# Hashed attention with two feed-forward blocks on one core: two weight slices converted at the attention's end, token differences in 2 KB halves, layer 3's first weight sums made in layer 2

## The chip, the cores and the metric

The kernel runs on one core of one Trainium2 chip. The metric is the device time of one execution in microseconds (us), the median over several runs; lower is better.

## The reference, cut to what matters

Everything is computed at fp32 accuracy. An attention over 16 heads (768 positions, 64 wide), in which a query sees only the keys of its hash bucket, gives the tokens `x` (1536 x 512); then four dense layers follow:

```
attn = softmax(where(q_bucket == k_bucket, q @ k.T / 8, -1e9)) @ v      # 2 x 8 heads
x = attn.transpose(0, 2, 1, 3).reshape(1536, 512)
h = max(max(x @ w1, x @ w2), x @ w3)          # layer 1: three 512 x 768
x = h @ w_out                                 # layer 2: 768 x 512
h = x @ w_in                                  # layer 3: 512 x 2048
g = where(h >= 1, h, where(h <= -1, 0, (h + 1)**2 / 4))
out = g @ w_out2                              # layer 4: 2048 x 512
```

## The kernel before, in words

**Matrix products.** An fp32 factor is held as two fp32r parts, hi and lo, and a product is three matmuls (hi·hi, hi·lo, lo·hi). A tile of 128 output features x 512 tokens with 256 inputs is therefore 6 matmuls of 128x512. Tokens lie in three blocks c = 0, 1, 2 of 512. PSUM banks come from a rotation of seven, `b0` to `b5` and `u_ps` (`bank`, `free`); the eighth, `pj_ps`, is scratch for the weights. Every engine takes its instructions in the order in which the program wrote them; an instruction that waits holds up all that stand behind it in its queue.

**Weights.** They arrive as 8-byte floats, in slices of 128 x 512 (512 KB), numbered in order of use: 0 to 17 for layer 1, 18 to 25 for layer 2 (384 wide), from 26 on for layers 3 and 4 in turn, two and two. `w_steps` converts one slice in steps: load of slice n+2 on SP (L196), Square on ACT (L211), four integer operations on DVE (L213, L218, L222, L226) that leave an fp32 number, on ACT the cast that makes hi (L234). The lo part is a subtraction on POOL (`w_low`, L268), issued when the next slice begins or when the slice is asked for. `w_tick(k)` makes k such steps; the calls of `w_tick`, strewn over the matrix work, are what sets the place of the steps in each queue. Of the raw 8-byte tiles there are two (`wr`), of the fp32 ones two (`wg2`).

**Pairs.** Slices 4 to 17 and those of layer 3 are taken two at a time by `pair_units`, which gets two slices x two blocks of tokens with seven products for eight, Strassen's way. It needs four sums of quarters of the two weight slices (s3, s2, s1, s4: `sr`, L245 to L250 on DVE), split into hi (ACT, L256) and lo (POOL, L258) by `sums_parts`, and four differences of tokens T1 to T4 (`x_d`; T4 overwrites a part of `x_hl`). When the next slice is the second of a pair and sums of an earlier pair are still to be split, `w_tick` stops; `w_state["open"]` says up to which pair sums may be split. Within a pair the matmuls come in groups of 6: product a; two groups of a plain block q; f = s3·T3; b += s2·T2 on top of a copy of a (L1056, ACT); a second product onto a; q; b += s1·T1; q; d; e. Between them ACT copies f to `x7` (L1067), DVE adds d = b + x7 (L1072), which must be through before s1 goes onto b, and ACT copies b to e (L1082) and to y (L1084), the first of which must be through before the product e.

**Order around the change.** A planner places the attention's work; at its end (some 195 to 207 us) hand-written code finishes the last pair of heads: row sums to `rt` (ACT, L594), `rt` to DRAM by a DMA from ACT's queue (L599), back as `rb` on all rows (SP, L605), the rows multiplied (`xr`, L614, DVE), then `x_hl` hi (L623, ACT) and lo (L627, DVE). Meanwhile PE runs the first units of layer 1 on the finished batch. Nine single units of layer 1 follow (`todo`, L1125 on; each ends in a copy or a maximum `h`, L967, L969), between which the 14 `steps` of the token differences run: four sums of two 128x1024 pieces (two on POOL, two on DVE, L1104), then `less` (DVE, L1027), casts (ACT, L1020) and lo parts (L1023, POOL or DVE). Then come the seven pairs `LEFT`, and layer 2: 12 units of 18 matmuls, whose results go straight to `x_hl` and to the token differences of layer 3 (L1163 to L1178). From 405.6 us on layers 3 and 4 run interleaved, pair i of layer 3 with the slices of pair i-1 of layer 4 (L1235), one `w_tick(2)` after each group of layer 3; g is made of r by ACT and DVE (L1201 to L1203), its hi by ACT (L1212), its lo by POOL (L1213).

Lines that carry another number after the change, in the rows of its order: L234 becomes L238, L256 L261, L594 L604, L599 L609, L605 L615, L1056 L1068, L1067 L1079, L1072 L1084, L1082 L1094, L1084 L1096, L1201 to L1212 become L1240 to L1251.

Of the kernel before, what the change touches and what calls it, by code (L numbers as in the profile page):

```python
# [8 lines left out]
F32 = mybir.dt.float32  # L9
# [104 lines left out]
def lsh_attention_moe_kernel(  # L114
# [85 lines left out]
    def w_steps(n):  # L200
# [16 lines left out]
        g2 = w_p.tile([128, 512], I32, tag="wg2", name="wg2", bufs=2)[:, 0:cols]  # L217
# [11 lines left out]
        yield  # L229
# [4 lines left out]
        nc.scalar.copy(out=w[:, 0, 0:cols], in_=f32(g2))  # L234
        splits[n] = w
        low_todo.append((n, w, g2, cols))
        g2s[n] = f32(g2)
# [28 lines left out]
    def w_low():  # L266
        for n, w, g2, cols in low_todo:
            nc.gpsimd.tensor_tensor(out=w[:, 1, 0:cols], in0=f32(g2), in1=f32(w[:, 0, 0:cols]), op=ALU.subtract)  # L268
        low_todo.clear()

    def w_tick(count=1):
        for _ in range(count):
            sums_tick()
            if w_state["gen"] is None:
                n = w_state["done"]
                if n >= NSL:
                    w_low()
                if n >= NSL or n >= w_state["base"] + (WBUFS if w_state["more"] else WEARLY):
                    return
                if n in pair_at and sums_todo:  # L280
                    return
                w_state["gen"] = w_steps(n)
# [37 lines left out]
    def attention(mlp_steps):  # L320
        with ExitStack() as ax, ExitStack() as sx:
# [610 lines left out]
    def mlp():  # L932
        with ExitStack() as mx:
# [11 lines left out]
            def free(b, full=True):  # L945
                banks.append(b[0])
                (whole.add if full else whole.discard)(b[0])
# [6 lines left out]
            def tok(c):  # L954
                return slice(c * TCH, (c + 1) * TCH)
# [48 lines left out]
            w_state["sums"] = mx.enter_context(tc.tile_pool(name="s", bufs=4))  # L1004
# [4 lines left out]
            low = [None] * 4  # L1009
            lk, rk, c0, c1 = slice(0, 2), slice(2, 4), tok(0), tok(1)  # L1010

            def lows():
                for m in (2, 1, 0, 3):
                    low[m] = w_state["sums"].tile([128, 2, TCH], F32, tag="s", name="raw")

            def d_parts(m, rows, eng):
                to = [x_d[:, m, p, rows] if m < 3 else x_hl[:, p, rows, c1] for p in range(2)]

                def hi():
                    nc.scalar.copy(out=to[0], in_=low[m][:, rows])  # L1020

                def lo():
                    eng.tensor_tensor(out=to[1], in0=low[m][:, rows], in1=f32(to[0]), op=ALU.subtract)  # L1023
                return hi, lo
# [12 lines left out]
            def pair_units(m, out_):  # L1037
# [6 lines left out]
                for x, (t, i) in dict(s3=(0, 0), s2=(0, 1), s1=(1, 0), s4=(1, 1)).items():  # L1044
                    left[x] = [tuple(s_[t][:, p, i, k * 128:(k + 1) * 128] for p in range(2)) for k in range(2)]
# [55 lines left out]
            with tc.tile_pool(name="h", bufs=1) as h_p:  # L1101
                hh["t"] = h_p.tile([128, 6, 2, NT], F32R, name="hh")
                lows()
# [3 lines left out]
                cut = [d_parts(m, lk, eng) for m, eng in enumerate((nc.gpsimd, nc.gpsimd, nc.vector, nc.gpsimd))]  # L1107
                steps = [
                    lambda: add(nc.gpsimd, 0, lk, c0),
                    lambda: add(nc.gpsimd, 3, rk, c0),  # L1110
                    lambda: add(nc.vector, 2, lk, c1),
                    lambda: add(nc.vector, 1, rk, c1),
                    lambda: less(low[0], low[2], low[0]),
                    lambda: less(low[2], low[1], low[2]),
                    cut[2][0],
                    lambda: less(low[1], low[1], low[0]),
                    cut[2][1],
                    cut[0][0],
                    cut[1][0],
                    lambda: less(low[3], low[3], low[1]),  # L1120
                    cut[1][1],
                    cut[0][1],
                ]

                todo = [(j, w, c) for j, w in ((0, 0), (0, 1), (0, 2), (1, 0)) for c in range(NTC) if (j, w, c) not in early or c]  # L1125
                for n, (j, w, c) in enumerate(todo):
                    l1(j, w, c, slice(S - TCH, TCH) if (j, w, c) in early else slice(0, TCH), 2 if n < 4 else 3)
                    for _ in range(3):
                        if steps:
                            steps.pop(0)()  # L1130
                    if not steps:
                        w_state["open"] = 1
                    if n + 1 == len(todo) or todo[n + 1][1] != w:
                        w_done(("1", j, w))
                for fn in steps:
                    fn()
                cut[3][0]()
                cut[3][1]()
# [11 lines left out]
                lows()  # L1150
                for j in range(4):
                    wts = [w_get(("2", j, g)) for g in range(2)]
                    i = j % 2
                    for c in ((2, 0, 1) if j == 0 else range(NTC)):
# [10 lines left out]
                        elif c == 0:  # L1165
                            raw = low[0 if j < 2 else 3][:, i]
# [3 lines left out]
                        elif j < 2:  # L1170
                            nc.scalar.copy(out=low[2][:, i], in_=pb)
                            less(low[0][:, i], low[2][:, i], low[0][:, i])
                        else:
                            t1, t2, t3, t4 = (t[:, i] for t in low)
                            one = slice(i, i + 1)
                            cut = [d_parts(m, one, eng) for m, eng in enumerate((nc.gpsimd, nc.gpsimd, nc.vector, nc.gpsimd))]
                            nc.scalar.copy(out=t2, in_=pb)
                            nc.scalar.copy(out=xh, in_=pb)  # L1178
                            less(t3, t2, t3)
                            cut[2][0]()  # L1180
                            less(xl, t2, f32(xh))
                            cut[2][1]()
                            less(t2, t2, t1)
                            less(t4, t4, t2)
                            for m in (0, 1, 3):
                                for fn in cut[m]:
                                    fn()
                        free(b)
                        w_tick(4)
                        if j == 3 and c == 1:  # L1190
                            w_state["open"] = len(LEFT) + 2
                    w_done(("2", j, 1))

            with tc.tile_pool(name="g", bufs=1) as g_p:
# [57 lines left out]
                for i in range(9):  # L1252
# [68 lines left out]
```

## Time and profile before

| | us |
|---|---|
| runs shown, median (lowest, highest) | 673.12 (672.02, 676.54) |
| the profiled execution | 671.09 |
| its span in the trace | 669.3 |
| granted TensorE clock, mean over the span | 0.987 of full speed |

The rows below come from the profiled execution. Its span starts with the first instruction; 1.8 us of the execution lie outside it. A matmul of 128x512 at full clock follows the one before after 227 ns (6 take 1.36 us, as the starts of consecutive groups in the trace show).

### The profile page before, as it was taken

The numbers are of one execution on the slowest core, as the hardware profiler recorded it, in microseconds if no ns is written. First come the engines' busy times: TensorE is split into PE (matmuls) and PEld (weight loads), VectorE is DVE, ScalarE is ACT, GpSimd is POOL, SyncE is SP. The second block draws the span as 40 slices with busy tenths as digits, with TensorE's granted clock in tenths as the row PEclk, the third lists the DMA queues.
The fourth block names the chain that finished last, engine by engine and source line by source line (L and its number), as shares of the span: only waits on it lengthen the run. The fifth ranks groups of instructions, "written<-read, shape, count | busy, mean of one in ns | idle before, by whom it ended". The sixth has DMA issues, their size and how long they took to land.

```text
span 669.3 us, 11587 instructions
## 1 busy us (share of the span) xinstructions
PE 645.2 (96%) x4323; PEld 513.4 (77%) x4323; DVE 495.6 (74%) x803; ACT 396.6 (59%) x740; POOL 352.8 (53%) x313
## 2 busy tenths in 40 slices
PE   7999999999999899889999998799999999999998
PEld 5668777778867677768888886588888888888886
DVE  5788989999863899878844477655786969696554
ACT  7687877887782344555443246778748374646440
POOL 6437547766322577657645255754646464645340
PEclk8999999999999989999999999899999999999999
DMA  6857787786333012231211211221211212121004
GB/s 189 224 122 185 198 213 182 199 247 153 92 112 81 32 64 95 94 95 55 71 49 47 64 63 59 68 94 64 64 63 64 89 37 94 36 92 63 1 0 189
DMA packets 27857, 66.99 MB, mean 100 GB/s; under 512 B 4165, under 2 KB 9125, under 8 KB 27801
## 3 DMA queue, kind: packets, MB, share of 16 engines
q1 hardware_dynamic: 27488, 66.21, 33.9%
q8 instruction: 34, 0.56, 0.3%
q14 instruction: 23, 0.18, 0.1%
q10 hardware_dynamic: 312, 0.04, 0.0%
HBM read 46.17 MB, written 3.19 MB: 74 GB/s over the span
## 4 chain that ended last, share of the span: by engine, by line
PE 79%; DVE 12%; ACT 4%; issue 3%; DMA 1%; POOL 1%; DVEq 0%; ACTq 0%; SPq 0%; POOLq 0%
PE b L308 24%; PE b L1235 18%; PE u_ps L308 7%; PE s_ps L449 6%; PE t_ps L482 5%; PE u_ps L543 5%; PE s_ps L452 5%; PE u_ps L510 3%; DVE raw L1027 2%; PE u_ps L1235 2%; PE pj_ps L425 2%; DVE pj_ps L213 1%; DVE wg L226 1%; DVE wg L218 1%; DVE pj_ps L222 1%
## 5 line engine op out<-in xcount | busy, mean ns | idle before, releaser
L459 DVE TENSOR_SCALAR_CACHE_REDUCE p<-s_ps 128x768 f32<-128x768 f32 x96 | 89.7, 951 | 13.3 <-PE s_ps L452 10.0
L474 ACT ACTIVATE p<-p,nm 128x768 f32<-128x768 f32 x96 | 89.7, 936 | 7.2 <-DVE p L459 6.7
L1213 POOL TENSOR_TENSOR g<-r,g 128x512 fp32r<-128x512 f32 x48 | 62.7, 1306 | 37.9 <-ACT g L1212 37.7
L449 PE MATMUL s_ps<-lo,q 128*128 128x384 f32 x192 | 72.5, 378 | 3.1 <-POOL lo L416 2.0
L308 PE MATMUL b<-x_d,s 128*128 128x512 f32 x270 | 68.6, 398 | 6.4 <-DVE u_ps L1072 2.6
L1235 PE MATMUL b<-wx,g 128*128 128x512 f32 x264 | 67.5, 393 | 4.5 <-ACT wx L234 3.3
L308 PE MATMUL b<-x_hl,wx 128*128 128x512 f32 x264 | 65.7, 393 | 1.5 <-ACT x_hl L1163 1.2
L308 PEld LDWEIGHTS b<-x_d,s 128*128 128x128 f32 x270 | 51.2, 192 | 19.6 <-DVE u_ps L1072 3.4
L452 PE MATMUL s_ps<-hi,q 76*128 76x384 f32 x192 | 66.1, 344 | 0.0
L213 DVE SCALAR_TENSOR_TENSOR pj_ps<-pj_ps,wr 128x512 f32<-128x512 f32 (+1 forms) x55 | 37.2, 677 | 37.5 <-ACT pj_ps L211 37.5
L1235 PE MATMUL b<-w,g 128*128 128x512 f32 (+1 forms) x264 | 64.6, 384 | 0.0
L234 ACT CAST wx<-wg 128x512 fp32r<-128x512 f32 (+1 forms) x32 | 19.4, 605 | 73.3 <-DVE wg L226 73.3
L1235 PEld LDWEIGHTS b<-wx,g 128*128 128x128 f32 x264 | 49.8, 189 | 15.7 <-ACT wx L234 3.7
L268 POOL TENSOR_TENSOR wx<-wg,wx 128x512 fp32r<-128x512 f32 (+1 forms) x32 | 40.7, 1273 | 39.3 <-ACT wx L234 36.1
L308 PEld LDWEIGHTS b<-x_hl,wx 128*128 128x128 f32 x264 | 50.1, 190 | 12.7 <-ACT x_hl L1163 1.7
L308 PE MATMUL b<-x_hl,w 128*128 128x512 f32 (+1 forms) x282 | 59.5, 363 | 0.0
L1242 DVE TENSOR_TENSOR acc<-b,acc 128x512 f32<-128x512 f32 (+1 forms) x77 | 51.6, 677 | 8.9 <-PE b L1235 8.9
L1235 PEld LDWEIGHTS b<-w,g 128*128 128x128 f32 x264 | 48.9, 188 | 9.9
L308 PEld LDWEIGHTS b<-x_hl,w 128*128 128x128 f32 x282 | 48.0, 189 | 8.8 <-issue 0.6
L449 PEld LDWEIGHTS s_ps<-lo,q 128*128 128x128 f32 x192 | 36.7, 191 | 21.3 <-DVE p L459 8.6
L492 ACT COPY pt<-t_ps 128x768 f32<-128x768 f32 (+1 forms) x59 | 41.0, 706 | 17.0 <-PE t_ps L482 14.7
L268 POOL TENSOR_TENSOR w<-wg,w 128x512 fp32r<-128x512 f32 (+1 forms) x26 | 33.0, 1269 | 29.9 <-ACT w L234 26.8
(154 smaller groups left out, 1495.9 us busy)
## 6 DMA issues: line engine op xcount, KB each, us to landing
wr<-in_w SPq DMA_DIRECT2D x48, 512.0 KB
r<-in_kq SPq DMA_DIRECT2D x15, 384.0 KB
q<-hi SPq DMA_DIRECT2D x15, 384.0 KB
v<-in_v SPq DMA_DIRECT2D x21, 256.0 KB
rb<-d SPq DMA_DIRECT2D x16, 192.0 KB
wr<-in_w SPq DMA_DIRECT2D x8, 384.0 KB
q<-lo SPq DMA_DIRECT2D x15, 192.0 KB
lo<-hi SPq DMA_DIRECT2D x15, 192.0 KB
```

The source lines that it names most:

```text
L213: nc.vector.scalar_tensor_tensor(out=f32(g), in0=f32(g), scalar=TINY_SQ, in1=f32(high), op0=ALU.is_ge, op1=ALU.mult)
L268: nc.gpsimd.tensor_tensor(out=w[:, 1, 0:cols], in0=f32(g2), in1=f32(w[:, 0, 0:cols]), op=ALU.subtract)
L308: nc.tensor.matmul(out=outp, lhsT=w_[a], rhs=x_[b_], start=(begins and i == 0 and jj == 0), stop=(ends and i == n - 1 and jj == 2), skip_g ...
L449: nc.tensor.matmul(out=o, lhsT=hd["qa"][:, qs], rhs=hd["lo"][:, ks], start=True, stop=False)
L452: nc.tensor.matmul(out=o, lhsT=hd["qb"][0:76, qs], rhs=hd["hi"][0:76, ks], start=False, stop=True)
L459: nc.vector.tensor_scalar(out=p.rearrange("p (a k) -> p a k", a=2), in0=s_ps[bank.at][:, :, 0:HALF], scalar1=MASKED, scalar2=MASKED, op0=A ...
L474: nc.scalar.activation(out=p, in_=p, func=ACTF.Exp, scale=-1.0, bias=tl[n]["nm"], accum_out=sums_of(h // 2)[:, c:c + 1],)
L482: nc.tensor.transpose(out=t_ps[:, half, j * 128:(j + 1) * 128], in_=tl[n]["p"][:, kt * 128:(kt + 1) * 128], identity=ident,)
L492: copy(out=grp[g][:, 3 * a:3 * b_, r * 128:(r + 1) * 128].rearrange("p (a j) q -> p a j q", a=b_ - a), in_=t_ps[:, a:b_, 0:HALF].rearrange ...
L1213: nc.gpsimd.tensor_tensor(out=lo, in0=r, in1=f32(hi), op=ALU.subtract)
L1235: nc.tensor.matmul(out=pb[:, cs], lhsT=gs[f][:, a, tsl], rhs=wt[:, b_, cs], start=(n == 0), stop=(n == len(terms) - 1),)
L1242: nc.vector.tensor_tensor(out=acc[:, t, cs], in0=pb[:, cs], in1=acc[:, t, cs], op=ALU.add)
```

## The change

It does five things.

1. `w_steps` is cut in `w_front` (load, Square, four DVE operations) and `w_back` (cast, sums). The fronts of slices 3 and 4 are issued at the attention's end, around `ahead_mm` and `ahead_copy`, ahead of the copy of `rt`; a third `wg2` tile holds the results.
2. The sums of weights are split in four pieces of 128x256 instead of two of 128x512, each with a tick of its own for hi and for lo.
3. The token differences of layer 1 are made in halves of 128x512 (2 KB a partition). A sum hi + lo is an ACT copy of hi into a PSUM bank and a DVE addition of lo with that bank as operand (L1120, L1121 of the new file); POOL adds nothing any more. The banks come from the rotation.
4. In layer 2 the last four blocks c = 1 and c = 0 read the result from its bank, without a copy; the casts and lo parts of T2, T1 and T4 are put off until after block c = 2; `open` is raised at the end of rows j = 2 and 3, so that layer 3's first pair may split its sums during layer 2.
5. In the first pair of layer 3 `w_tick(3)` takes the place of `w_tick(2)`.

The diff, cut to its core:

```diff
-    def w_steps(n):
+    def w_front(n):
         w_load(n + 2)
...
-        g2 = w_p.tile([128, 512], I32, tag="wg2", name="wg2", bufs=2)[:, 0:cols]
+        g2 = w_p.tile([128, 512], I32, tag="wg2", name="wg2", bufs=3)[:, 0:cols]
...
     def sums_parts(m, sr):
-        s_ = sums_w[m] = [w_state["sums"].tile([128, 2, 2, 256], F32R, tag="s", name="s") for _ in range(2)]
-        for i in range(2):
-            nc.scalar.copy(out=s_[i][:, 0], in_=sr[:, 2 * i:2 * i + 2])
+        s_ = sums_w[m] = []
+        for i in range(4):
+            t = w_state["sums"].tile([128, 2, 256], F32R, tag="s", name="s")
+            s_.append(t)
+            nc.scalar.copy(out=t[:, 0], in_=sr[:, i])
             yield
-            nc.gpsimd.tensor_tensor(
-                out=s_[i][:, 1], in0=sr[:, 2 * i:2 * i + 2], in1=f32(s_[i][:, 0]), op=ALU.subtract
-            )
+            nc.gpsimd.tensor_tensor(out=t[:, 1], in0=sr[:, i], in1=f32(t[:, 0]), op=ALU.subtract)
+            if i < 3:
+                yield
...
             pair_recip(last)
+            for _ in w_front(WEARLY):
+                pass
             ahead_mm(2, 4)
             ahead_copy()
+            for _ in w_front(WEARLY + 1):
+                pass
...
-                add = lambda eng, m, kk, c: eng.tensor_tensor(
-                    out=low[m], in0=f32(x_hl[:, 0, kk, c]), in1=f32(x_hl[:, 1, kk, c]), op=ALU.add
-                )
...
+                    def whole_of(kk, c, out_=None):
+                        b = bank()
+                        nc.scalar.copy(out=b[1], in_=f32(x_hl[:, 0, kk, c]))
+                        nc.vector.tensor_tensor(
+                            out=b[1] if out_ is None else out_, in0=b[1], in1=f32(x_hl[:, 1, kk, c]), op=ALU.add
+                        )
...
+                    whole_of(2 + i, c1, t2)
+                    yield
+                    less(t3, t2, b[1])
...
-                            nc.scalar.copy(out=t2, in_=pb)
                             nc.scalar.copy(out=xh, in_=pb)
-                            less(t3, t2, t3)
-                            cut[2][0]()
-                            less(xl, t2, f32(xh))
-                            cut[2][1]()
-                            less(t2, t2, t1)
+                            less(xl, pb, f32(xh))
+                            less(t3, pb, t3)
+                            hi, lo = cut(2, i, nc.vector)
+                            hi()
+                            less(t2, pb, t1)
+                            lo()
                             less(t4, t4, t2)
-                            for m in (0, 1, 3):
-                                for fn in cut[m]:
-                                    fn()
+                            late += [fn for m in (1, 0, 3) for fn in cut(m, i)]
                         free(b)
                         w_tick(4)
-                        if j == 3 and c == 1:
-                            w_state["open"] = len(LEFT) + 2
+                        if c == 2 and late:
+                            for fn in late:
+                                fn()
+                            late.clear()
+                            w_state["open"] = len(LEFT) + j - 1
...
                         if x == "3":
-                            w_tick(2)
+                            w_tick(2 if i else 3)
```

ACT's queue at the attention's end, before: the copies that finish the last heads, then the copy of `rt`, its DMA `d`, the copy of the second sums, and only after the casts of `x_hl` the Square of slice 3 (`pj_ps<-wr`).

```order
L234 CAST w<-wg_2647 128x512
L523 COPY u<-t_ps 128x2x6x32
L521 COPY u<-u_ps 128x6x32
L521 COPY u<-pj_ps 128x6x32
L532 COPY h_2774<-s_ps_122 128x512
L594 COPY rt<-pj_ps 12x128
L599 DMA d<-rt 12x128
L575 COPY u<-u_ps 64x384
L967 COPY h_2811<-b_2798 128x256
L623 CAST x_hl<-xr 128x384 x2
```

The same place now: the Squares of slices 3 and 4 (`wg<-wr`) stand ahead of the copy of `rt`.

```order
L238 CAST w<-wg_2647 128x512
L533 COPY u<-t_ps 128x2x6x32
L531 COPY u<-u_ps 128x6x32
L531 COPY u<-pj_ps 128x6x32
L211 ACTIVATE wg<-wr 128x512
L542 COPY h_2783<-s_ps_122 128x512
L211 ACTIVATE wg<-wr 128x512
L604 COPY rt<-pj_ps 12x128
L609 DMA d<-rt 12x128
L585 COPY u<-u_ps 64x384
L982 COPY h_2829<-b_2816 128x256
L633 CAST x_hl<-xr 128x384 x2
```

Two Squares moved ahead of `rt` and of all that hangs on it.

SP's queue at the same time, before, from the load of slice 3 on (`uc`, `u`, `uo` belong to the last heads' sums):

```order
L196 DMA wr<-in_w 128x1024
L537 DMA uc<-u 64x768
L570 DMA uc<-uo 64x384
L571 DMA u<-uo 64x384
L605 DMA rb<-d 64x768 x2
L196 DMA wr<-in_w 128x1024 x14
```

And now:

```order
L196 DMA wr<-in_w 128x1024
L547 DMA uc<-u 64x768
L580 DMA uc<-uo 64x384
L581 DMA u<-uo 64x384
L196 DMA wr<-in_w 128x1024 x2
L615 DMA rb<-d 64x768 x2
L196 DMA wr<-in_w 128x1024 x12
```

The loads of slices 4 and 5 moved ahead of `rb`.

ACT's queue in layer 3's first pair, before, from the copy of f to the copy e (`s<-sr` splits sums, r and g belong to the blocks' outputs, the Square `pj_ps<-wr` is slice 30's); slice 29's Square and cast stand ahead of this stretch, before and now:

```order
L1067 COPY x_4346<-b_2863 128x512
L256 CAST s<-sr 128x512
L211 ACTIVATE pj_ps<-wr 128x512
L1201 ACTIVATE r<-u_ps,half_sb 128x512
L1202 ACTIVATE r<-r 128x512
L1212 CAST g<-r 128x512
L256 CAST s<-sr 128x512
L1082 COPY b_2908<-b_2798 128x512
```

And now, the same stretch (`w` and `wx` are the casts of slices 30 and 31):

```order
L1079 COPY x_4431<-b_2851 128x512
L261 CAST s<-sr 128x256
L211 ACTIVATE pj_ps<-wr 128x512
L261 CAST s<-sr 128x256 x2
L238 CAST w<-wg_4443 128x512
L1240 ACTIVATE r<-b_2816,half_sb 128x512
L1241 ACTIVATE r<-r 128x512
L1251 CAST g<-r 128x512
L261 CAST s<-sr 128x256
L211 ACTIVATE pj_ps<-wr 128x512
L238 CAST wx<-wg_4480 128x512
L1094 COPY b_2867<-b_2831 128x512
```

Two whole conversions, Square to cast (slices 30 and 31), now lie between the copy of f and the copy e; before it was one Square, whose cast followed behind the copy e.

## Rows read from the trace of the kernel before

**Rows 1.** The page: busy us, share, instructions of each engine; POOL's costliest group.

```profile
PE 645.2 (96%) x4323; PEld 513.4 (77%) x4323; DVE 495.6 (74%) x803; ACT 396.6 (59%) x740; POOL 352.8 (53%) x313
...
L1213 POOL TENSOR_TENSOR g<-r,g 128x512 fp32r<-128x512 f32 x48 | 62.7, 1306 | 37.9 <-ACT g L1212 37.7
```

**Rows 2.** Stretches: bounds; engines' busy us (instructions); PEclk; DMA share; GB/s.

```profile
230.00:235.00 5.00, 2.25 (x7) 1.50 (x7) 4.50 (x6) 3.78 (x5) 1.55 (x1) 0.76 0.32 107
235.00:240.00 5.00, 5.00 (x14) 3.92 (x13) 4.96 (x6) 0.85 (x2) 4.64 (x2) 0.56 0.00 0
244.00:297.00 53.00, 46.98 (x201) 36.96 (x200) 46.73 (x72) 27.03 (x49) 34.72 (x27) 1.00 0.28 90
405.00:413.00 8.00, 5.91 (x25) 4.02 (x23) 5.25 (x7) 5.60 (x11) 5.16 (x5) 1.00 0.13 49
428.00:439.00 11.00, 6.46 (x18) 4.48 (x18) 6.67 (x10) 8.43 (x16) 6.93 (x6) 0.69 0.29 95
```

**Rows 3.** PE's waits: who waited for whom, us in total, times, longest us.

```profile
PE b L1235 <- ACT wx L234: 3.3, 1, 3.3
PE b L308 <- DVE u_ps L1072: 2.6, 2, 2.2
...
PE u_ps L308 <- ACT wx L234: 1.9, 1, 1.9
```

**Rows 4.** DVE's timeline: start us, us, line, operation [idle before].

```profile
209.37 0.56 DVE L576 COPY uc<-u_ps 64x384 f32<-64x384 f32 x1 [8.12 <-ACT u L575]
...
214.02 1.03 DVE L614 TENSOR_TENSOR xr<-u,rb 128x384 f32<-128x384 f32 x2 [1.29 <-DMA rb<-d]
...
215.30 1.02 DVE L627 TENSOR_TENSOR x_hl<-xr,x_hl 128x384 fp32r<-128x384 f32 x2
...
221.03 1.28 DVE L1104 TENSOR_TENSOR raw<-x_hl 128x1024 f32<-128x1024 f32 x1
...
223.55 2.10 DVE L1104 TENSOR_TENSOR raw<-x_hl 128x1024 f32<-128x1024 f32 x1
```

**Rows 5.** SP's queue at the attention's end; slice 5's load; GB/s, 230 to 236.

```profile
190.81 0.32 SPq L599 DMA_DIRECT2D d<-rt  x1
192.41 1.10 SPq L605 DMA_DIRECT2D rb<-d  x2
...
209.38 1.11 SPq L605 DMA_DIRECT2D rb<-d  x2
210.53 31.08 SPq L196 DMA_DIRECT2D wr<-in_w  x3
...
231.25 66.81 SPq L196 DMA_DIRECT2D wr<-in_w  x12
...
GB/s 0 0 0 0 0 0 0 0 0 0 0 0 0 0 137 109 109 27 300 355 437 437 410 410 355 328 82 0 0 0 55 0 0 0 0 0 0 0 0 0
```

**Rows 6.** ACT's timeline at the attention's end: start us, us, line, operation, idle before.

```profile
206.38 0.56 ACTq L599 DMA_DIRECT2D d<-rt  x1
...
218.96 0.38 ACT L967 COPY h<-b 128x256 f32<-128x256 f32 x1 [3.37 <-PE b L308]
```

**Rows 7.** POOL's timeline: its two additions for the token differences.

```profile
221.18 6.73 POOL L1104 TENSOR_TENSOR raw<-x_hl 128x1024 f32<-128x1024 f32 x2
```

**Rows 8.** PE's timeline: layer 3's first group; f and s2 of pair two.

```profile
405.60 1.52 PE L308 MATMUL u_ps<-x_hl,wx 128*128 128x512 f32 x6
...
434.80 4.13 PE L308 MATMUL b<-x_d,s 128*128 128x512 f32 x12
```

**Rows 9.** ACT's timeline at the start of layer 3.

```profile
411.79 0.62 ACT L211 ACTIVATE pj_ps<-wr 128x512 f32<-128x512 f32 x1
...
415.82 0.62 ACT L234 CAST w<-wg 128x512 fp32r<-128x512 f32 x1 [2.14 <-DVE wg L226]
...
420.23 0.58 ACT L1082 COPY b<-b 128x512 f32<-128x512 f32 x1
...
432.14 0.53 ACT L1056 COPY b<-b 128x512 f32<-128x512 f32 x1
```

More of the change, by code (lines that the diff above doesn't have):

```diff
@@ L943, in bank, with free @@
                 return n, at_bank[n]
-            def free(b, full=True):
+            def free(b, full=None):
                 banks.append(b[0])
-                (whole.add if full else whole.discard)(b[0])
+                if full is not None:
+                    (whole.add if full else whole.discard)(b[0])
             def flush():
@@ L1008, in mlp, with lows, cut @@
             x_d = d_p.tile([128, 3, 2, 2, TCH], F32R, name="x_d")
[L1009 to L1024, printed above, removed]
+            low = {}
+            c0, c1 = tok(0), tok(1)
+            def lows(order):
+                for m, i in order:
+                    low[m, i] = w_state["sums"].tile([128, TCH], F32, tag="s", name="raw")
+            def cut(m, i, eng=nc.gpsimd):
+                hi, lo = (x_d[:, m, p, i] if m < 3 else x_hl[:, p, i, c1] for p in range(2))
+                return (
+                    lambda: nc.scalar.copy(out=hi, in_=low[m, i]),
+                    lambda: eng.tensor_tensor(out=lo, in0=low[m, i], in1=f32(hi), op=ALU.subtract),
+                )
             def less(o, a, b_):
@@ L1102, in mlp @@
                 hh["t"] = h_p.tile([128, 6, 2, NT], F32R, name="hh")
-                lows()
-                add = lambda eng, m, kk, c: eng.tensor_tensor(
-                    out=low[m], in0=f32(x_hl[:, 0, kk, c]), in1=f32(x_hl[:, 1, kk, c]), op=ALU.add
-                )
[L1107 to L1123, printed above, removed]
+                lows(((2, 0), (1, 0), (0, 0), (2, 1), (1, 1), (0, 1), (3, 0), (3, 1)))
@@ new lines, in d_steps @@
+                def d_steps(i):
+                    def whole_of(kk, c, out_=None):
[3 more added lines that the diff above has]
+                            out=b[1] if out_ is None else out_, in0=b[1], in1=f32(x_hl[:, 1, kk, c]), op=ALU.add
+                        )
+                        if out_ is not None:
+                            free(b)
+                        return b
+                    t1, t2, t3, t4 = (low[m, i] for m in range(4))
+                    b = whole_of(i, c1)
+                    yield
+                    whole_of(2 + i, c1, t2)
+                    yield
+                    less(t3, t2, b[1])
+                    yield
+                    hi, lo = cut(2, i, nc.vector)
+                    hi()
+                    whole_of(i, c0, t1)
+                    yield
+                    less(t1, b[1], t1)
+                    free(b)
+                    yield
+                    lo()
+                    yield
+                    less(t2, t2, t1)
+                    yield
+                    for fn in cut(1, i):
+                        fn()
+                    b = whole_of(2 + i, c0)
+                    yield
+                    less(t4, b[1], t2)
+                    free(b)
+                    yield
+                    for fn in cut(0, i):
+                        fn()
+                    yield
@@ L1125, in mlp, with d_tick @@
+                steps = [d_steps(0), d_steps(1)]
+                def d_tick(count):
+                    for _ in range(count):
+                        if steps:
+                            steps.append(steps.pop(0))
+                            if next(steps[-1], 0) == 0:
+                                steps.pop()
+                    if not steps:
+                        w_state["open"] = 1
                 todo = [(j, w, c) for j, w in ((0, 0), (0, 1), (0, 2), (1, 0)) for c in range(NTC) if (j, w, c) not in early or c]
@@ L1127, in mlp @@
                     l1(j, w, c, slice(S - TCH, TCH) if (j, w, c) in early else slice(0, TCH), 2 if n < 4 else 3)
[L1128 to L1132, printed above, removed]
+                    d_tick(3)
                     if n + 1 == len(todo) or todo[n + 1][1] != w:
                         w_done(("1", j, w))
[L1135 to L1138 removed]
+                d_tick(99)
+                for i in range(2):
+                    for fn in cut(3, i):
+                        fn()
                 w_state["open"] = 2
@@ L1149, in mlp @@
                 ht = hh["t"]
-                lows()
+                lows((m, i) for i in range(2) for m in (2, 1, 0, 3))
+                late = []
                 for j in range(4):
```

36 lines of the change are left out of this document (21 added, 15 removed).

## The prediction

> **What bounds the kernel now.** I read the page's busy shares first, then PE's waits, then the stretches in which these lie, and last the queues of the engines that PE waits for. PE is busy 96% of the span, ACT 59% and POOL 53% [rows 1]: the end is set by PE, and only what makes PE wait counts. A matmul of 128x512 needs 227 ns at full clock, so the stretches give the loss [rows 2]: 230 to 240 us holds 7 + 14 matmuls, 4.8 us of work in 10, 5.2 lost; 244 to 297 (pairs 0 to 2 of layer 1) 201, 45.6 of 53, 7.4 lost; 405 to 413 25, 5.7 of 8, 2.3 lost; 428 to 439 18, 4.1 of 11, 6.9 lost. Together 21.8 us. The reader is to see that in the first and the last the clock fell too: PE waited 1.9 us for a weight cast by ACT, and 3.3 us for another [rows 3], and the granted clock behind was 0.56 of full in 235 to 240, which is the lower of TensorE's two levels (1.2 of 2.4 GHz). The rest of pairs 0 to 2 is waits for DVE's addition d, 2.6 us in two [rows 3], and for copies that stand late in ACT's queue. These 21.8 us are all that the change can win; what it can lose is not bounded so, since every queue is in order.
>
> I followed each engine's queue of the changed program from 200 to 300 us and from 390 to 445, gave each instruction the duration of its kind, and started it when its queue and its inputs were ready. The three places that decide:
>
> **The attention's end.** The front of slice 3 costs nothing: DVE is idle 8.12 us ahead of 209.37 [rows 4], and its Square and four operations take about 4 (below). The front of slice 4 is another matter, since its Square needs a load that is not there. That load was issued at 210.53, behind the two of `rb`, and now takes their place, some 209.4 [rows 5]. A load of a slice takes 3.0 us: slice 5's is issued at 231.25, and the last large slice of the GB/s row (its 39 values share 6 us) is the 27th, at 234.2 [rows 5]. So the Square starts about 212.5, and behind it in ACT's queue stand the copy of `rt` and its DMA. `d`, issued at 206.38 before [rows 6], goes out at 213.6 (0.6 for the Square, 0.3 for the copy, some hand-over): 7.2 later. `rb` follows 1.6 us after `d` (190.81 to 192.41 an earlier time) [rows 5], so at 215.2 instead of 209.38, 5.8 later. From there `xr` takes 4.6 us (209.38 to 214.02) [rows 5, 4], the cast comes next, and the lo part ends 2.3 after `xr` starts (216.32 less 214.02) [rows 4]: 222.2 instead of 216.3. PE needs this for the unit whose output ACT copies at 218.96 [rows 6], in the last quarter of its 12 matmuls of 256 columns, at about 218.5. Before there were 2.2 us in hand; now PE waits 3.3 (the hi part is needed first, and the last lo matmuls come a little later). If `rb` took as long behind `d` as the 3.0 us from 206.38 to 209.38, the wait would be 4.7; if the Square found its load early, none: 0 to 4.7, taken 3.3, since the nearest row of the same transfer is the 1.6. A wait of that size is followed by the lower clock in [rows 2]: of the 5.2 lost in 230 to 240 PE sat idle for 2.75 (10 less 2.25 and 5.00), and 2.5 were the clock. I take 2.5 again.
>
> **Layer 1.** In return slices 3 and 4 are ready, and the 5.2 us of 230 to 240 go. Pair 0, which began at 244 [rows 2], then starts at 244.0 - 5.2 + 3.3 + 2.5 = 244.6, 0.6 later. The four additions of 128x1024, of which two were on POOL, become eight ACT copies and eight DVE additions of 128x512, cheap for both. But ACT's eight copies stand behind two casts and POOL's queue holds four lo parts of x_d and x_hl ahead of the first pieces of s, each 1.3 us [rows 1]. By the walk s3's lo is ready at 254.4. f is due after three groups, 244.6 + 4.1 = 248.7, and waits 5.7 us; after that pairs 0 to 2 lose little more, some 0.6 us, because the sums come in pieces and the slices are ahead: 6.3 instead of 7.4, a gain of 1.1. Net of layer 1: +0.5 us won. Bounds: all of the 5.2 and 3 of the 7.4 won with no wait at 218 (+8), or the whole 7.4 kept and the wait 4.7 (-4).
>
> The rule that bears on it: DVE's addition took 1.28 us where it began 0.15 before POOL's, and the same instruction 2.10 two instructions later [rows 4], with POOL's two at work from 221.18 to 227.9 [rows 7]. The Trainium skill (SBUF — State Buffer, Who interferes with whom) has a DVE instruction with two SBUF inputs contend with a GpSimd instruction that reads SBUF, and one with at most one SBUF input not. By it the halves with a bank as operand run at their undisturbed time, DVE's part of the token differences gets some 3.3 us shorter (0.8 for each of four such instructions beside POOL), and if DVE set the time of s3 the sum would come out 4 us slower in place of 7.5; the rows fit the rule, but POOL's own queue is later than DVE's here.
>
> **The start of layer 3.** Count from 405.60, the first group of its first pair [rows 8]. The 2.3 us of 405 to 413 go: the casts are spread over layer 2 and s is cut before. Slice 29's Square starts at +3.1 instead of 411.79, which is +6.2 [rows 9, 8]. From there three ticks a group are the trouble. From a Square to its cast four DVE operations must pass, 4.0 us (411.79 to 415.82) [rows 9], and the cast now stands in ACT's queue with little between, so ACT idles. Cast 29 at +7.1; behind it two r, the copy x7 and a piece of s, 0.5 to 0.6 each [rows 9]; Square 30 at +9.3; DVE adds d behind two of its operations, at +12.2 to +12.9. The product s1 is due after 7 groups, 7 x 1.36 = +9.5, so PE waits 3.3. Cast 30 at +13.3; r, r, g and a piece of s; Square 31 at +16.2; cast 31 at +20.2; the copy e from +20.8 to +21.3. Product e is due after 10 groups and that wait, 13.6 + 3.3 = +16.9: another wait of 4.4. Before, the copy e was made at 420.23, +14.6 [rows 9], and e was due at 13.6 + 2.3 = +15.9: no wait. So e ends at +22.7 and did at +17.3: 5.4 later.
>
> Then the copies e and y, Square 32 and its cast at +25.9, three times r, r, g (1.8 each time), Square 33, its cast at +35.8, and behind it the copy of a for the second pair, at +36.4, in place of 432.14, +26.5 [rows 9]. The product s2 waits for it (some 5 us) and ends at +38.3; before it ended with the row of 434.80, at 438.9, +33.3 [rows 8], after all of its waits. The 6.9 us of 428 to 439 are thus more than replaced: 5.0 later. The lower clock follows such a wait for some microseconds; the stretch before had its share inside the 6.9, so I add 2.5 (the same row as above) for a second. If the cast came 1.6 us sooner each time, the second pair would be 3.4 late and without a second drop; if the copies were never late, the stretch would win 2.3 + 6.9 = 9.2. Net -7.5 to -8, bounds -10 to +9. From the second pair on the casts of 128x256 add two ACT instructions a pair, with some 2 us to spare at the copy e; nothing.
>
> **Sum.** +0.5 - 5.0 - 2.5 to -3.0: 7.5 us slower. On the profiled execution 671.1 + 7.5 = 678.6; the median of the runs is 673.12, 2.0 above it, so the median after is 680.6.
>
> **Rivals.**
> *It works as meant.* The place is the copy e of layer 3's first pair: if it comes by +15.9 nothing waits there, since the DVE operations between Square and cast run ahead of ACT. Then 2.3 + 6.9 us are won there, 5.2 in layer 1, less the 3.3 at 218: 11 us, 662; without that wait 659. For it: ACT is only 59% busy and DVE 74% [rows 1]. The Trainium skill (Perfetto Trace Analysis, Optimizing Scalar/DVE Operations) advises to break up instructions where ACT and DVE are not saturated and still cause bubbles on others, which is what the pieces do; by it alone this would be the likeliest case. Against it: it takes a Square-to-cast time of about 2 us, and the row has 4.0.
> *It cancels.* The load of slice 4 is early enough, or `rb` quick enough, that PE loses nothing at 218, so layer 1 wins its 5.2 + 0.5, and layer 3 loses 5 to 6: 673, within 1%. For it: 2.2 us were in hand at 218. Against it: 5.8 us must be found.
> *It is worse.* The wait at 218 is 4.7, the clock is low for longer behind all three waits (2.5 more each for two), 1.4 + 5 on top: 687. For it: 2.75 us of waits cost 5.2 in 230 to 240 [rows 2].
>
> **How the numbers follow.** A measurement of this kernel tells about 1% (6.7 us) from no change. My forecast has 0.50: its own range is 675 to 686, and 0.08 of the 0.50 lie under +6.7. It cancels 0.22, it works 0.18, it is worse 0.10. Faster by over 1%: 0.18. Within 1%: 0.22 + 0.08 = 0.30. Slower: 0.42 + 0.10 = 0.52. The range leaves out the better half of the second case, and the end of the worst: 664 to 688.
>
> **What the profile after would show.** Right: `d` issued about 213.6 and a wait of PE on `x_hl` near 218 to 222, low clock behind it; no wait on a weight cast in 228 to 240; PE waiting for s3's lo in pair 0; ACT idle about 3 us ahead of each cast of slices 29 to 31 and PE waiting on the copy e and on the copy of a in the second pair. Wrong: `d` out before 209, or the copy e inside 16 us of the start of layer 3's first pair. Without the first the time is about 675, without the second about 670, without either 660.

## The result, and the profile after

The changed kernel takes 683.09 us (median of 4 runs, 681.33 to 683.92) beside 672.63 for the kernel before in the same session: ratio 1.014, 95% interval 1.0095 to 1.0184. It is slower, by 10.5 us where 7.5 were forecast (680.6). The profiled execution (683.92, span 682.1) is 12.8 us longer than that of before; it is the slowest of its four runs, and that of before is faster than any of the runs beside it, so the traces show some 2 us more than the medians. Where this arises is seen at places that both traces have: pair 0 of layer 1 starts at 246.6 instead of 244.1, pair 3 at 299.25 instead of 296.8, layer 3 at 409.86 instead of 405.60, and s2 of its second pair ends at 449.7 instead of 438.9. The lag is thus 2.5, 2.5, 4.3 and 10.8 us, and 12.8 at the end; 0.9 of it is there already in the attention, ahead of any changed instruction that PE waits for; executions of one program differ by more there (its last products start at 207.43 before, at 207.10 and 209.22 in experiments 11 and 5, with the same instructions up to there).

PE's waits in the trace after, which answer to [rows 3] (who waited for whom, us in total, times, longest):

```profile
PE b L318 <- DVE b L1084: 6.5, 5, 3.6
PE b L318 <- ACT b L1068: 4.9, 1, 4.9
PE b L318 <- POOL s L263: 3.2, 1, 3.2
PE b L318 <- ACT x_hl L633: 3.0, 1, 3.0
PE b L318 <- ACT b L1094: 2.7, 1, 2.7
```

Both waits for weight casts in [rows 3] are gone; in their place stand longer waits for d (6.5 in all, 4.5 before) and waits for the copies of a and e, for the sums and for the attention's last rows. The stretches, as in [rows 2]:

```profile
220.00:230.00 10.00, 7.12 (x21) 5.42 (x22) 5.12 (x10) 4.87 (x10) 3.77 (x3) 0.66 0.08 34
230.00:240.00 10.00, 9.61 (x51) 8.10 (x51) 9.24 (x17) 3.97 (x8) 0.00 (x0) 1.00 0.12 33
250.00:260.00 10.00, 5.54 (x17) 3.78 (x16) 4.69 (x7) 6.51 (x16) 9.70 (x10) 0.83 0.22 62
410.00:425.00 15.00, 11.45 (x49) 9.10 (x48) 9.73 (x16) 8.00 (x17) 9.47 (x9) 0.96 0.11 37
425.00:450.00 25.00, 16.34 (x58) 12.02 (x57) 15.26 (x23) 17.21 (x33) 14.07 (x12) 0.84 0.27 84
```

The stretch 230 to 240 is healed, and 220 to 230, 250 to 260 and 410 to 450 are worse. Two of these before:

```profile
220.00:230.00 10.00, 10.00 (x56) 8.43 (x54) 9.51 (x7) 0.98 (x2) 7.92 (x3) 1.00 0.01 2
...
250.00:260.00 10.00, 8.47 (x36) 6.59 (x36) 8.84 (x14) 4.55 (x8) 6.26 (x4) 1.00 0.32 105
```

ACT's timeline at the attention's end, to be read against [rows 6]:

```profile
206.03 0.59 ACT L542 COPY h<-s_ps 128x512 f32<-128x512 f32 x1
214.09 0.67 ACT L211 ACTIVATE wg<-wr 128x512 f32<-128x512 f32 x1 [7.47 <-DMA wr<-in_w]
214.66 0.24 ACT L604 COPY rt<-pj_ps 12x128 f32<-12x128 f32 x1
214.93 0.56 ACTq L609 DMA_DIRECT2D d<-rt  x1
```

ACT stands idle for 7.47 us, and the row says for what: slice 4's load. `d` goes out at 214.93 instead of 206.38. The start of layer 3 in PE's timeline, for [rows 8]:

```profile
409.86 1.52 PE L318 MATMUL b<-x_hl,wx 128*128 128x512 f32 x6
...
423.09 2.45 PE L318 MATMUL b<-x_d,s 128*128 128x512 f32 x6 [3.55 <-DVE b L1084]
...
431.78 1.65 PE L318 MATMUL b<-x_hl,s 128*128 128x512 f32 x6 [2.72 <-ACT b L1094]
...
446.75 2.93 PE L318 MATMUL b<-x_d,s 128*128 128x512 f32 x6 [4.89 <-ACT b L1068]
```

ACT's timeline of the same time, for [rows 9]:

```profile
416.50 0.62 ACT L238 CAST w<-wg 128x512 fp32r<-128x512 f32 x1 [2.94 <-DVE wg L226]
...
424.39 0.62 ACT L238 CAST w<-wg 128x512 fp32r<-128x512 f32 x1 [3.35 <-DVE wg L226]
...
430.62 0.62 ACT L238 CAST wx<-wg 128x512 fp32r<-128x512 f32 x1 [3.02 <-DVE wg L226]
431.14 0.58 ACT L1094 COPY b<-b 128x512 f32<-128x512 f32 x1
...
445.59 0.62 ACT L238 CAST wx<-wg 128x512 fp32r<-128x512 f32 x1 [2.94 <-DVE wg L226]
446.12 0.58 ACT L1068 COPY b<-u_ps 128x512 f32<-128x512 f32 x1
```

Ahead of each cast ACT idles 3 us for DVE's last operation, and the copies that PE needs (e at 431.14, a at 446.12) stand behind the casts. Six matmuls behind the waits for d and for a take 2.45 and 2.93 us instead of 1.52; the granted clock there was 0.63 of full on the mean (423.1 to 425.3) and 0.50 (446.75 to 449.48), the lower of TensorE's two levels (1.2 of 2.4 GHz).

### The profile page after: what moved, and what is told of

It reads as the page before. It is cut to its first block, busy times and chain, and to the rows that moved or that the text cites. A ratio compares the mean times of both kernels' runs of the same rounds, so it can differ in the third digit from the quotient of the medians.

```text
span 682.1 us, 11682 instructions
## 1 busy us (share of the span) xinstructions
PE 650.1 (95%) x4323; PEld 515.8 (76%) x4323; DVE 491.6 (72%) x814; ACT 402.3 (59%) x780; POOL 351.1 (51%) x344
## 3 DMA queue, kind: packets, MB, share of 16 engines
q1 hardware_dynamic: 27488, 66.21, 33.3%
## 4 chain that ended last, share of the span: by engine, by line
PE 34%; DVE 19%; ACT 9%; issue 4%; DVEq 0%; ACTq 0%
PE b L318 21%; PE b L1274 8%; PE u_ps L318 3%; DVE pj_ps L213 3%; DVE acc L1281 3%; DVE wg L218 3%; DVE pj_ps L222 3%; DVE wg L226 2%; ACT r L1240 2%; PE u_ps L1274 2%; ACT g L1251 2%; DVE sr L250 1%; ACT pj_ps L211 1%; ACT r L1241 1%; DVE h L984 1%
## 5 line engine op out<-in xcount | busy, mean ns | idle before, releaser
L318 PE MATMUL b<-x_hl,w 128*128 128x512 f32 (+1 forms) x348 | 80.6, 382 | 3.8 <-ACT x_hl L633 3.0
L318 PE MATMUL b<-x_hl,wx 128*128 128x512 f32 x330 | 80.9, 392 | 0.0
L318 PEld LDWEIGHTS b<-x_hl,w 128*128 128x128 f32 x348 | 63.3, 194 | 17.2 <-ACT x_hl L633 3.2
L318 PEld LDWEIGHTS b<-x_hl,wx 128*128 128x128 f32 x330 | 62.8, 190 | 13.3
L1274 PE MATMUL b<-w,g 128*128 128x512 f32 (+1 forms) x243 | 59.3, 387 | 0.0
L1274 PE MATMUL b<-wx,g 128*128 128x512 f32 x225 | 56.7, 391 | 1.1 <-POOL g L1252 0.6
L1242 DVE SCALAR_TENSOR_TENSOR r<-r,b 128x512 f32<-128x512 f32 x36 | 24.7, 685 | 41.4 <-ACT r L1241 40.0
L263 POOL TENSOR_TENSOR s<-sr,s 128x256 fp32r<-128x256 f32 x60 | 45.4, 773 | 16.3 <-ACT s L261 12.5
L1274 PEld LDWEIGHTS b<-w,g 128*128 128x128 f32 x243 | 45.4, 190 | 9.3
L1281 DVE TENSOR_TENSOR acc<-b,acc 128x512 f32<-128x512 f32 (+1 forms) x68 | 45.2, 676 | 8.9 <-PE b L1274 8.9
```

The lines of the kernel that those rows point to most:

```text
L263: nc.gpsimd.tensor_tensor(out=t[:, 1], in0=sr[:, i], in1=f32(t[:, 0]), op=ALU.subtract)
L318: nc.tensor.matmul(out=outp, lhsT=w_[a], rhs=x_[b_], start=(begins and i == 0 and jj == 0), stop=(ends and i == n - 1 and jj == 2), skip_g ...
L1274: nc.tensor.matmul(out=pb[:, cs], lhsT=gs[f][:, a, tsl], rhs=wt[:, b_, cs], start=(n == 0), stop=(n == len(terms) - 1),)
L1281: nc.vector.tensor_tensor(out=acc[:, t, cs], in0=pb[:, cs], in1=acc[:, t, cs], op=ALU.add)
```

## The experiments

Times are medians; the kernel before, run beside them, had 673.2 to 673.4. The first four share a session, and so do the next four and the last three; the change was measured in one of its own, so that a difference from it of 1 or 2 us is not told from none by the intervals.

**1. Slice 4's front taken out of the attention's end.**

```diff
             ahead_copy()
-            for _ in w_front(WEARLY + 1):
-                pass
```

> The change without the early front of slice 4 (its steps run in the ticks again; slice 3's front stays at the attention's end). Theory (the Square of slice 4 holds up the copy of rt in ACT's queue): d goes out near 207 instead of 214.9, PE's wait of 3.0 us for x_hl and the low clock behind it go, 5 to 6 us less than the change (677 to 678); a new wait on slice 4's cast in 230 to 240 may give back up to 2. Rival (x_hl was late for another reason, such as the loads ahead of rb on SP): d early but rb still late, no gain over 1 us, 682 to 683.

681.86 us, ratio to before 1.0126 (1.0092 to 1.016): 1.2 less than the change, which had 1.014. `d` went out at 207.26, and the wait on `x_hl` is gone, so the mechanism is as the theory says; its price is not. Pair 0 starts 5.6 us sooner (240.9) and waits longer there. PE's timeline of this run:

```profile
248.34 1.21 PE L318 MATMUL b<-x_d,s 128*128 128x512 f32 x4 [2.57 <-POOL s L263]
252.48 1.22 PE L318 MATMUL b<-x_d,s 128*128 128x512 f32 x2 [2.93 <-ACT b L1066]
254.13 2.07 PE L318 MATMUL b<-x_d,s 128*128 128x512 f32 x4 [0.43 <-POOL s L263]
```

The sums and the copy of a come when ACT, DVE and POOL get to them; PE that arrives early waits there. Pair 1 starts only 3.7 us sooner (264.5 instead of 268.2), and 3.2 of this are left at the end of the span. That the medians show 1.2 is in part scatter: this trace is the fastest of its four runs, that of the change the slowest of its four. Against experiment 2, which has the change's program up to layer 3, pair 0 starts 3.5 us sooner, pair 1 2.8 and layer 3 1.8. No wait for slice 4's cast came; at 229.7 PE waits 1.3 us for a bank that an addition of the token differences (L1119 here) still reads.

**2. Two ticks in layer 3's first pair.**

```diff
-                            w_tick(2 if i else 3)
+                            w_tick(2)
```

> The change with two ticks a group in layer 3's first pair, as before it. Theory (the third tick puts whole conversions, Square to cast, ahead of the copies that PE needs): the copy e comes 12 to 13 us after the pair's start instead of 21.3, the waits on d (3.6), e (2.7) and the second pair's copy of a (4.9) go, a wait of 1 to 3 us on layer 4's second weight cast takes their place as before the change; 8 to 11 us less than the change, 672 to 675. Rival (the sums in four pieces and the earlier open fill ACT's queue, the tick is a bystander): the copy e stays later than 17 us and the gain is under 3, 680 or more.

672.60 us, ratio to before 0.9989 (0.996 to 1.0019): 10.5 less than the change, as the theory says. The pair starts at 408.45 and the copy e is made 11.4 us later (12 to 13 were expected); ACT's timeline:

```profile
419.81 0.58 ACT L1094 COPY b<-b 128x512 f32<-128x512 f32 x1
```

PE's waits:

```profile
PE b L1274 <- ACT wx L238: 3.1, 1, 3.1
...
PE b L1274 <- POOL wx L273: 1.3, 1, 1.3
```

The waits of before at layer 4's second slice ([rows 3]: 3.3) are back. The row of f and s2 of the second pair, which answers to the last of [rows 8]:

```profile
434.55 4.24 PE L318 MATMUL b<-x_d,s 128*128 128x512 f32 x12
```

It ends 30.3 us after the pair's start; in the change s2 ended after 39.8, before after 33.3.

**3. T4's lo parts on DVE.**

```diff
-                    for fn in cut(3, i):
+                    for fn in cut(3, i, nc.vector):
```

> The change with the two lo parts of T4 in layer 1 on DVE instead of POOL. Theory (s3's lo part stands behind four lo parts in POOL's queue while DVE is idle for 6 us): s3's lo part 2.5 us earlier, PE's wait of 3.2 us in pair 0 falls to 1 or less, with the clock behind it 2.5 to 5 us less than the change, 678 to 680.5. Rival (ACT's casts of the sums set the time): the wait is put down to ACT and stays, under 1 us gained.

680.99 us, ratio to before 1.0123 (1.0082 to 1.0164): 2.1 less than the change, a little short of the theory's range and above the rival's. PE's wait for POOL fell from 3.2 to 1.2; the wait of 1.3 us for ACT's cast of the sums ahead of it stayed, and a wait of 1.1 us for d came behind it. The median alone does not show the gain: the interval overlaps the change's, and in this trace the wait on `x_hl`, ahead of the edit, was 1.2 instead of 3.0. Experiment 2 is the fairer neighbour, as its pair 0 starts at the same time (244.4, here 244.5): layer 3 starts there at 408.45, here at 406.60. Two single executions thus put the edit at 1.9 us.

**4. All three**, with slice 4's front not left out but put behind the last lo part of `x_hl`; to the edits of 2 and 3 comes

```diff
             ahead_copy()
-            for _ in w_front(WEARLY + 1):
-                pass
...
             for half in range(2):
                 norm_lo(last, half, nc.vector)
+            for _ in w_front(WEARLY + 1):
+                pass
```

> All three: slice 4's front behind the last lo part of x_hl, two ticks, T4's lo parts on DVE. Theory: the three gains add up, 15 to 19 us less than the change, 664 to 668, which is 5 to 8 under the kernel before. Rival (the waits hide behind one another): 670 to 674, no better than before.

668.83 us, ratio to before 0.9929 (0.9902 to 0.9957): faster than before, but 14.3 less than the change where 15 to 19 were expected. Experiments 1 to 3 had given 1.2, 10.5 and 2.1, together 13.8: the gains add up, though the front is here moved and not left out, and it is the price of the front that was put too high.

**5. The third tick alone, in the kernel before.**

```diff
-                            w_tick(2)
+                            w_tick(2 if i else 3)
```

> The kernel before with three ticks a group in layer 3's first pair, nothing else. Theory (the third tick alone does the harm, whatever the sums are): two casts, each 4 us behind its Square, stand ahead of the copy e, which comes later than 20 us after the pair's start instead of 14.6; 7 to 12 us slower than before, 680 to 685. Rival (the tick harms only with the sums in four pieces and the earlier open): within 3 us of before.

683.09 us, ratio 1.0145 (1.0116 to 1.0173): 9.9 slower than before, the same median as the whole change. The theory holds: the third tick does its harm without the sums in four pieces and without layer 2's new order. The copy e is made 24.3 us after the pair's start. PE's timeline of this run shows the three waits of the change in other sizes; the pair starts at 407.37:

```profile
423.93 2.93 PE L308 MATMUL b<-x_d,s 128*128 128x512 f32 x6 [3.94 <-DVE b L1072]
...
432.25 1.65 PE L308 MATMUL b<-x_hl,s 128*128 128x512 f32 x6 [1.34 <-ACT b L1082]
...
447.30 2.93 PE L308 MATMUL b<-x_d,s 128*128 128x512 f32 x6 [4.91 <-ACT b L1056]
```

From the pair's start to the end of s2 it is 42.86 us here and 33.33 before, 39.82 in the change and 30.34 in experiment 2. Up to there the third tick thus costs 9.5 us in either kernel, and the rest of the change wins 3.0 with the tick and without it.

**6. Two ticks and no early front at all**: experiments 1 and 2 together, and

```diff
             pair_recip(last)
-            for _ in w_front(WEARLY):
-                pass
```

> The change with two ticks in layer 3's first pair and without both early fronts. It tells what the fronts are worth: against the run with two ticks (672.6). Theory A (they hide two conversions that PE waits for in 230 to 240): a wait on a weight cast comes back there, 3 us or more slower, 675 to 679. Theory B (PE's early gain is given back in pair 0, whose sums come when ACT, DVE and POOL have made the token differences): within 2 us, 671 to 674.5.

670.51 us, ratio 0.9963 (0.9946 to 0.998), beside 0.9989 (0.996 to 1.0019) with the fronts: no gain from them, perhaps a loss (the intervals overlap, and the median is half a us below theory B's range). Theory A falls: no wait for a weight cast came back in 230 to 240. What came is a wait of 2.1 us, at 229.9, for a bank that the token differences hold (L1117 here), and 3.0 us in all for the sums in pair 0.

**7. Pair 0's sums opened early**, on top of experiment 4 (and the buffers `low` handed out in the order 2, 2, 1, 1, 0, 0).

```diff
                     b = whole_of(2 + i, c0)
+                    if i:
+                        w_state["open"] = 1
                     yield
```

> The run with all three edits (668.8), with pair 0's sums allowed to be split while the token differences still run (open raised after the third difference, the buffers in another order). Theory B goes on: what holds f in pair 0 is the time at which ACT begins to cast the sums, 10 us after DVE had them ready; the waits of 1.25 and 1.2 us before f and the clock of 0.88 behind them go, 2 to 4 us less, 664.5 to 667. Rival (the casts put earlier hold up the differences as much): within 1.5 us of 668.8.

668.11 us, 0.7 less than experiment 4: the rival's range. In the trace the waits for the sums are gone, as the theory had it, and waits of 1.7 us for the copy of a and 1.5 for d stand behind them in pair 0. The profiled executions differ by 2.3 us in span (663.9 and 666.2), the medians by 0.7; the gain is not shown.

**8. Four ticks after one group alone**, on top of experiment 7. It is the eighth group, product s1, behind which the copies e and y stand; the expectation below calls it the ninth.

```diff
-                            w_tick(2)
+                            w_tick(4 if i == 0 and n == 10 else 2)
```

> As the run with the sums opened early, with four ticks instead of two after the ninth group of layer 3's first pair alone, behind the copy e. Theory (ticks harm ahead of the copy e and help behind it, since layer 4's second weight cast then stands ahead of one r, r, g): the waits of 3.1 and 1.6 us at the first slice of layer 4 fall by 2 to 3 us in all, with less low clock behind, 2 to 4 us less, 661 to 664. Rival (ACT is full there and the wait only moves to the copy of a in the second pair): no change.

667.28 us, ratio to before 0.9911 (0.988 to 0.9942): the lowest median. The waits at layer 4's second slice fell by less than expected, PE's waits of this run:

```profile
PE b L1276 <- POOL wx L273: 1.6, 1, 1.6
PE b L1276 <- ACT wx L238: 1.4, 1, 1.4
...
PE b L318 <- ACT b L1094: 0.9, 1, 0.9
```

3.1 and 1.2 in experiment 7 became 1.4 and 1.6, some 1.4 less in all, and the second pair gives it back: 0.9 for its copy e and 0.5 for an output and d. This is the rival, with another copy than it named. The time is 0.8 less, inside the spread of either.

**9, 10. Experiment 8 with slice 3's front only** (the two lines added in experiment 4 go again), **and with none** (the two lines of experiment 6 go as well).

> As the run with late ticks (667.3), with the front of slice 3 alone, none of slice 4. If the front of slice 4 only brings PE earlier to pair 0, where it waits for the sums anyway, this is within 1.5 us of 667.3; if slice 4 is then missed between 228 and 240, 2 us or more slower.

> As the run with late ticks, without both fronts. With the sums opened early pair 0 is less of a backstop, so the fronts should now be worth something: 1 to 4 us slower than 667.3 (668 to 671). If it is faster, as it was without the early sums (670.5 against 672.6), the fronts harm by themselves: 664 to 666.5.

670.85 (0.9971, 0.9951 to 0.999) and 670.77 (0.9966, 0.9944 to 0.9988): both 3.5 slower than experiment 8, which ran in another session, and the intervals lie above its own (the second by a hair). With the sums open early and its Square behind the DMA of `rt`, slice 4's front is worth 3.5 us; slice 3's front alone is worth nothing that shows. It is not that slice 4 is missed: neither trace has a wait of PE for a weight cast in 228 to 240 (the second has 0.6 us for a lo part at 240.8). PE waits for the sums again in both (2.6 and 2.1 us), and for a bank of the token differences (1.3 and 2.1, where experiment 8 has 0.4).

**11. The late ticks alone, in the kernel before**: the edit of experiment 8.

> The kernel before with four ticks instead of two after the ninth group of layer 3's first pair, nothing else. By the theory (ticks help behind the copy e) PE's waits of 3.3 and 1.3 us at layer 4's first slice fall by 2 to 3 us: 669 to 671.5, the plain gain of moving two steps, where the change's extra tick on all groups cost 10. Rival (the wait moves to the second pair's copy of a): within 1 us of before.

673.58 us, ratio 1.0012 (0.9991 to 1.0033): the rival's time, by another copy. The two waits at layer 4's second slice fell from 4.6 to 3.1 in all (1.5 and 1.6 instead of 3.3 and 1.3), but the second pair's copy e, not its copy of a, came late and cost 1.2. PE's waits of this run:

```profile
PE b L1235 <- POOL wx L268: 1.6, 1, 1.6
PE b L1235 <- ACT wx L234: 1.5, 1, 1.5
...
PE b L308 <- ACT b L1082: 1.2, 1, 1.2
```

## Why the prediction was right, point by point

**The start of layer 3** carried the sum, and its mechanism came step by step. Counted from the pair's start, d was added from +12.5 to +13.2 (forecast +12.2 to +12.9), PE's wait 3.55 (3.3); the copy e at +21.3 (+20.8); the second pair's copy of a at +36.3 (+36.4), its wait 4.9 (some 5). Only the wait on e was smaller, 2.7 for 4.4, because PE ran at the lower clock behind d and reached e later; for the same reason s2 ended at +39.8, not +38.3. Experiments 2 and 5 show that the third tick is the cause of the loss: without it the change is as fast as before, and alone it costs before 9.9 us. The forecast had called the ticks "the trouble" and put 7.5 to 8 on the place, net of the 2.3 that were to be won at 405 to 413; the traces have 6.5 up to the end of s2 and 2.0 behind it, and 3.0 won beside the tick. The sum as written comes to 7.0 to 7.5, of which it took the upper end. Of layer 2's blocks only the two with c = 1 in rows j = 2 and 3 read their result from the bank; those with c = 0 keep their copy.

**The attention's end.** `d` went out 8.5 us late (forecast 7.2), since slice 4's load, issued at 210.17, let the Square start at 214.09, 3.9 later and not 3.0; slice 5's load was issued right behind it, but that this is the reason is not shown. PE waited 3.0 and 0.3 us (3.3). Behind it 12 matmuls of 512 columns took 5.1 us instead of 2.7 at a granted clock of 0.52 (224.26 to 229.36), about the 2.5 of the forecast. The wait scatters from one execution to the next: with the same code there it was 2.1 in experiment 2 and 1.2 in experiment 3. What this was worth is the term that was mis-sized. The prediction's last lines put the time without the late `d` at about 675, without the late copy e at about 670 and without either at 660, so 5.6 and 10.6 under the forecast. Experiments 1, 2 and 6 have 681.9, 672.6 and 670.5: the third tick is worth 10.5, as priced, and the late `d` 1.2 in the medians; part of what PE wins there it waits again in pair 0 (experiment 1).

**Layer 1** was to win 0.5, and in these two traces it lost 3.4. Pair 3 started 2.45 late, 1.5 without the 0.9 that the attention brought along: pairs 0 to 2 took 52.7 us before and after, where 1.1 less was forecast, pair 0 alone 21.6 instead of 18.1. A wait of 1.5 us for d in pair 4 (at 325.4), which the walk did not reach, made most of the rest of the 4.3. The size is not firm. Programs that are the same up to there start layer 3 at 405.60, 407.37 and 406.85 (before, experiments 5 and 11) and at 409.86 and 408.45 (the change, experiment 2), so between single executions the lag is 1.1 to 4.3. The mechanism of f was right: the first pieces of s stood behind POOL's four lo parts, and PE waited 1.3 + 3.2 for them where 5.7 was forecast, but the clock behind that wait was not in the sum. POOL's timeline after:

```profile
250.30 2.51 POOL L1035 TENSOR_TENSOR x_d<-raw,x_d 128x512 fp32r<-128x512 f32 x2 [1.15 <-ACT x_d L1034]
252.76 2.51 POOL L1035 TENSOR_TENSOR x_hl<-raw,x_hl 128x512 fp32r<-128x512 f32 x2
255.22 2.82 POOL L263 TENSOR_TENSOR s<-sr,s 128x256 fp32r<-128x256 f32 x4
```

**From the second pair on** "nothing" was forecast; two waits for d of 0.35 and 0.4 us (at 581 and 613) and the clock behind 446 (0.75 of full in 449 to 453) made most of the last 2 us of lag.

**The rule on the port.** By the Trainium skill (SBUF — State Buffer, Who interferes with whom) a DVE instruction with two SBUF inputs contends with one of POOL's that reads SBUF, and one with at most one such input does not. This trace agrees in the main: the additions with a bank as operand took 0.65 us each beside POOL's lo parts, while L250's sum of two SBUF operands, 0.42 us with POOL idle, took 1.40 beside it (L252's, at 261.51, took 0.41 beside it all the same):

```profile
226.47 1.30 DVE L1121 TENSOR_TENSOR b<-b,x_hl 128x512 f32<-128x512 f32 x2 [1.93 <-ACT b L1120]
...
240.36 0.42 DVE L250 TENSOR_TENSOR sr<-wg,sr 128x256 f32<-128x256 f32 x1
...
259.59 1.40 DVE L250 TENSOR_TENSOR sr<-wg,sr 128x256 f32<-128x256 f32 x1
```

It did not decide, as DVE had its sums ready at 241.4 and ACT began to cast them at 251.6. **The rivals:** "it works as meant" asked for a copy e inside 15.9 us; experiment 2 has it at 11.4, and still gains nothing over before: layer 3 starts 2.9 us late there, which is about what its start then wins. The Trainium skill (Perfetto Trace Analysis, Optimizing Scalar/DVE Operations) says that breaking up instructions may let work finish sooner where Scalar and Vector are not saturated but cause bubbles on other engines. No run has the pieces alone, nor the token differences or layer 2's order; the change without its third tick, which holds all three, shows no gain (0.9989), and what each is worth stays open. "It cancels" has the time of the change without its third tick, but by another way: PE still waits 2.1 us on `x_hl` there, and layer 3 loses nothing. "It is worse" did not come: the wait at 218 stayed at 3.3.

## What to carry to other kernels

In queues that run in order, the pace of a background conversion is a schedule: a step that waits for another engine should stand where the queue behind it is not needed, so pacing it faster can cost more than the wait that it was to remove. A prefetch whose first step waits for a load belongs behind the short instructions that start the critical transfer, never ahead of them. And a wait removed early in a stretch is worth only what the next place lets through at which the engine must wait anyway: here 5.6 us at the start of pair 0 were 3.7 one pair later, and 1.2 in the medians.

## What the runs showed that was not expected

The clock does not follow from the length of a wait alone. In experiment 8 waits of 1.4 and 1.6 us left the granted clock at 1.00 in 418 to 440; in experiment 11 waits of 1.5 and 1.6 us at the same place of the program went with 0.72 in 428 to 440. The stretch of experiment 8 (columns as in [rows 2]):

```profile
418.00:440.00 22.00, 18.47 (x78) 14.08 (x78) 16.62 (x26) 16.30 (x31) 15.14 (x14) 1.00 0.22 75
```

That of experiment 11:

```profile
428.00:440.00 12.00, 8.83 (x27) 6.52 (x26) 7.48 (x12) 9.26 (x17) 7.55 (x7) 0.72 0.26 87
```

Experiments 9 and 10, in which the engines run the same instructions in the same order from layer 2 on, show it closer still: PE waits 1.4 and 1.6 us at this place in both, and the 12 matmuls behind took 2.89 us in the one and 4.11 in the other:

```profile
432.21 2.89 PE L318 MATMUL b<-x_d,s 128*128 128x512 f32 x12
```

```profile
429.68 4.11 PE L318 MATMUL b<-x_d,s 128*128 128x512 f32 x12
```

Why the clock fell in the one and not in the other stays open. It may be part of why the removed waits moved the medians so little; that is not shown.
